# The order of issue planned in the source, w_in by column tile, batch 0's softmax with tokens on partitions

## The chip, the cores and the metric
One core of a Trainium2 chip. The metric is the device time of one execution in microseconds, as the median of several runs; a program that computes something else or in another precision does not count. The engines that matter are PE (TensorE, matmuls, with PEld for its weight loads), DVE (VectorE), ACT (ScalarE), POOL (GpSimd) and SP (SyncE, which issues most DMAs). Each executes its own list of instructions in order and waits on semaphores; the lists are fixed when the program is built.

## The reference
Eight batches b of 512 tokens x and 32 state rows, with 8 heads of width 64. First a two-way attention, then a feed-forward layer with squared ReLU over all 8 x (512 + 32) = 4352 rows of width 512, hidden width 2048; everything in float32.

```python
scores = scale * x @ state.T          # a = softmax over the 32 state rows, xread = a @ state
scores2 = scale * state @ x.T         # a2 = softmax over the 512 tokens, sread = a2 @ x
rows = concatenate([xread, sread])    # heads side by side: 512 columns
h = rows @ w_in; g = relu(h) ** 2; out = g @ w_out
```
The sums of the two softmaxes get 1e-9 before the division.

## The kernel before
**Precision.** A float32 operand of a big matmul is split into a high part (rounded to the type float32r, a copy on ACT, line 98) and a low part (the difference, a subtraction, line 99); three products hi x hi, lo x hi, hi x lo are added in PSUM. The weights come as 64-bit words; `singles` (lines 101 to 115) makes float32 of them with one ACT operation and three DVE operations per 128 x 512 tile.

**Work for the 512 tokens of a batch.** xread @ w_in is a @ (state @ w_in), so the kernel forms z = state @ w_in per head once for four batches together (`z_part`, L142: eight instructions on PE into two PSUM tiles `pz`, two ACT copies L157, one DMA to DRAM `zd`) and fetches the rows of a batch again (`z_fetch`, L179). For the first 6 of the 16 column blocks of batch 0 z is formed directly (`z_direct`, L165, three times 256 columns). A *unit* is one block `fc` of 128 hidden columns of one batch: `up` (L349) multiplies z by the softmax a (6 matmuls of 512 columns, L353) into `ph`, takes ReLU on ACT (L355), squares on ACT for the first ten units and on DVE after that (L357, L359) and splits into g_hi and g_lo; `down` (L366) multiplies by a 128 x 512 tile of w_out (12 matmuls, L379) into four PSUM tiles `po`. `mlp` (L342) runs `up(i)`, then `down(i - 2)`. After the last unit of a batch `po` goes to SBUF tiles `os_` (3 buffers) and out.

**Batch 0 in two visits.** `BOTH` (L67) orders the units: columns 0 to 5 of batch 0, then all of batch 1, then columns 6 to 15 of batch 0, then batches 2 to 7. The sums of the first visit go to DRAM and are added back in the second (L560 to L572).

**Softmax.** `attention_group` (L214), twice per batch (4 heads each): the scores of state row by token (`scores`, L241) lie with (head, state row) on partitions. `soft1` and `soft1b` turn 32 x 32 blocks with a DVE stream transpose (L262), so that the 32 state rows of a head lie along the free axis, take maximum, difference, exponential, sum, reciprocal and product (L274 to L284), turn back (L286) and split into a_hi, a_lo. Difference and product are on POOL for batches 0 to 2, on DVE from batch 3 on (`pool_early(b < 3)`); a_lo is on DVE for batch 0 and POOL after it. The other softmax, e2 (L263 to L268), is kept, and `turn` and `read` (L297, L312) form sread in `sr` two batches later. For batches from 2 on x is split too, low parts on POOL (L238, L294).

**Loads and weights.** 16 tiles of w_in (512 KB, 256 columns and half of the rows each, `z_load`) and 16 tiles of w_out (`wo_load`, L402) share four buffers `raw`; the low part of w_out is made on POOL (L412).

**Last part.** The 256 state rows of all batches go through the same layer with 16 units of half width (L579 to L609).

**Order.** Two lists of steps, `weights` and `reads`, are spread by counting: each has steps with due slots, and after each `up` and each `down` the class `Ahead` (L436) emits as many steps as the nearest due slot needs. The framework then schedules the emitted operations once more with its own timing model (`schedule_with_timeline_sim=True`, L639).

## Time and profile before
| | |
|---|---|
| time, median of 3 runs | 762.25 us (761.93 to 762.26) |
| profiled execution: time, span | 761.69 us, 759.9 us |
| PE busy, mean granted clock | 713.6 us (94%), 0.952 |
| DVE, ACT, POOL busy | 439.1 us (58%), 378.3 us (50%), 151.9 us (20%) |
| DMA | 79.00 MB, mean 104 GB/s |
| chain that ended last | PE 82%, DVE 9%, DMA 4%, ACT 2% |

The share of busy time is an average over stages that differ: some 110 us in which the weights come in, then batch after batch. Busy PE is not PE at full speed: the row of the granted clock says what share of the full clock it had. A line number such as L99 can be that of a helper (`split`, `singles`), so groups are told apart by the tiles they write.

### The profile page before, as it was taken

The numbers are of one execution on the slowest core, as the hardware profiler recorded it, in microseconds if no ns is written. First come the engines' busy times: TensorE is split into PE (matmuls) and PEld (weight loads), VectorE is DVE, ScalarE is ACT, GpSimd is POOL, SyncE is SP. The second block draws the span as 40 slices with busy tenths as digits, with TensorE's granted clock in tenths as the row PEclk, the third lists the DMA queues.
The fourth block names the chain that finished last, engine by engine and source line by source line (L and its number), as shares of the span: only waits on it lengthen the run. The fifth ranks groups of instructions, "written<-read, shape, count | busy, mean of one in ns | idle before, by whom it ended". The sixth has DMA issues, their size and how long they took to land.

```text
span 759.9 us, 9457 instructions
## 1 busy us (share of the span) xinstructions
PE 713.6 (94%) x3136; PEld 561.3 (74%) x3136; DVE 439.1 (58%) x729; ACT 378.3 (50%) x714; POOL 151.9 (20%) x170
## 2 busy tenths in 40 slices
PE   4899669999998999996999999999999999999997
PEld 2556447777885777764888888888888888888896
DVE  5999852334565432636477588478468544444453
ACT  4486664334555544644465565466446434533443
POOL 1333240000323120113223222223312211100000
PEclk9599769999997999995999999999999999999999
DMA  9577870033225333242132321141113201200101
GB/s 306 196 252 264 306 258 27 28 125 124 70 63 200 108 106 138 84 152 85 36 90 58 115 83 57 56 138 56 61 60 119 81 28 39 73 28 1 56 1 28
DMA packets 50368, 79.00 MB, mean 104 GB/s; under 512 B 6928, under 2 KB 32656, under 8 KB 50320
## 3 DMA queue, kind: packets, MB, share of 16 engines
q1 hardware_dynamic: 45520, 61.37, 25.0%
q10 hardware_dynamic: 4800, 17.04, 5.7%
q8 instruction: 24, 0.39, 0.2%
q14 instruction: 24, 0.20, 0.1%
HBM read 51.64 MB, written 26.74 MB: 103 GB/s over the span
## 4 chain that ended last, share of the span: by engine, by line
PE 82%; DVE 9%; DMA 4%; ACT 2%; issue 2%; POOL 0%; SPq 0%; DVEq 0%; ACTq 0%; POOLq 0%
PE po L379 47%; PE ph L353 25%; PE pz L151 4%; PE pr L316 2%; PE pst L257 1%; PE pq L247 1%; DMA w_raw<-w_in 1%; DVE wof L112 1%; DVE wof L108 1%; DVE wi L108 1%; DMA part<-os__634 1%; PE pt L304 1%; DVE wi L112 1%; DMA part<-os__646 1%; DMA sp_f<-stP 1%
## 5 line engine op out<-in xcount | busy, mean ns | idle before, releaser
L379 PE MATMUL po<-wo_hi,g_hi 128*128 128x512 f32 x544 | 219.2, 403 | 6.5 <-ACT g_hi L98 6.5
L379 PE MATMUL po<-wo_lo,g_hi 128*128 128x512 f32 x544 | 215.9, 397 | 0.0
L359 DVE TENSOR_TENSOR ph<-ph,r 128x512 f32<-128x512 f32 (+1 forms) x134 | 89.0, 665 | 178.5 <-ACT r L355 178.1
L355 ACT ACTIVATE r<-ph 128x512 f32<-128x512 f32 (+1 forms) x144 | 82.6, 576 | 193.6 <-PE ph L353 193.6
L379 PE MATMUL po<-wo_hi,g_lo 128*128 128x512 f32 x544 | 151.7, 394 | 0.0
L379 PEld LDWEIGHTS po<-wo_hi,g_hi 128*128 128x128 f32 x544 | 103.5, 190 | 33.9 <-ACT g_hi L98 7.8
L99 DVE TENSOR_TENSOR g_lo<-ph,g_hi 128x512 fp32r<-128x512 f32 (+1 forms) x144 | 94.5, 658 | 58.5 <-ACT g_hi L98 33.9
L379 PEld LDWEIGHTS po<-wo_lo,g_hi 128*128 128x128 f32 x544 | 103.7, 191 | 21.8 <-issue 0.3
L379 PEld LDWEIGHTS po<-wo_hi,g_lo 128*128 128x128 f32 x544 | 101.2, 188 | 22.3 <-issue 0.8
L98 ACT CAST g_hi<-ph 128x512 fp32r<-128x512 f32 (+1 forms) x144 | 81.0, 564 | 50.1 <-DVE ph L359 37.5
L99 POOL TENSOR_TENSOR xn_hl<-xn_raw,xn_hl 128x512 fp32r<-128x512 f32 x32 | 42.3, 1321 | 223.6 <-ACT xn_hl L98 223.6
L353 PE MATMUL ph<-a_hi,z_hi 128*128 128x512 f32 x256 | 85.4, 412 | 0.8 <-ACT a_hi L98 0.7
L353 PE MATMUL ph<-a_hi,z_lo 128*128 128x512 f32 x256 | 84.1, 411 | 0.0
L353 PE MATMUL ph<-a_lo,z_hi 128*128 128x512 f32 x256 | 82.7, 404 | 0.0
L151 PE MATMUL pz<-wi,st_z 64*128 64x256 f32 x256 | 63.2, 446 | 13.6 <-ACT z_stage L157 12.8
L151 PEld LDWEIGHTS pz<-wi,st_z 64*128 64x128 f32 x256 | 38.1, 207 | 37.0 <-ACT z_stage L157 18.8
L99 POOL TENSOR_TENSOR xt_hl<-xt_raw,xt_hl 128x512 fp32r<-128x512 f32 x24 | 31.5, 1312 | 161.7 <-ACT xt_hl L98 161.7
L353 PEld LDWEIGHTS ph<-a_hi,z_lo 128*128 128x128 f32 x256 | 50.9, 199 | 12.2 <-issue 0.7
L353 PEld LDWEIGHTS ph<-a_lo,z_hi 128*128 128x128 f32 x256 | 49.6, 195 | 12.8 <-issue 1.7
L353 PEld LDWEIGHTS ph<-a_hi,z_hi 128*128 128x128 f32 x256 | 48.6, 196 | 13.9 <-issue 1.6
L157 ACT COPY z_stage<-pz 128x512 f32<-128x512 f32 x64 | 36.5, 588 | 32.7 <-PE pz L151 30.1
L99 DVE TENSOR_TENSOR z_lo<-z_raw,z_hi 128x512 fp32r<-128x512 f32 x61 | 44.9, 735 | 8.3 <-ACT z_hi L98 8.3
(120 smaller groups left out, 706.7 us busy)
## 6 DMA issues: line engine op xcount, KB each, us to landing
zd<-z_stage ACTq DMA_DIRECT2D x32, 512.0 KB, 3.0
z_raw<-zd SPq DMA_DIRECT2D x244, 64.0 KB, 2.3
xt_raw<-xT SPq DMA_DIRECT2D x16, 512.0 KB, 3.6
w_raw<-w_in SPq DMA_DIRECT2D x16, 512.0 KB, 4.8
wo_raw<-w_out SPq DMA_DIRECT2D x16, 512.0 KB, 4.9
xn_raw<-xn SPq DMA_DIRECT2D x16, 512.0 KB, 3.8
part<-part SPq DMA_DIRECT2D x4, 256.0 KB, 3.2
st_z<-stT SPq DMA_DIRECT2D x4, 128.0 KB, 5.6
```

The lines of the kernel that those rows point to most:

```text
L98: nc.scalar.copy(out=hi, in_=src)
L99: eng_lo.tensor_sub(out=lo, in0=src, in1=hi.bitcast(F32))
L108: nc.vector.scalar_tensor_tensor(out=bits, in0=high, scalar=-0x80000000, in1=bits, op0=ALU.bitwise_and, op1=ALU.bitwise_or,)
L112: nc.vector.scalar_tensor_tensor(out=bits, in0=low, scalar=29, in1=bits, op0=ALU.logical_shift_right, op1=ALU.bitwise_or,)
L151: nc.tensor.matmul(pz[i][:, q, :], lhsT=st[G][own, cc, :], rhs=wi[own, k, cc, :], start=True, stop=True,)
L157: nc.scalar.copy(out=stage[:, :, i, :], in_=pz[i])
L247: nc.tensor.matmul(pq, lhsT=sp_hl[:, g, q].rearrange("p i n -> p (i n)"), rhs=v, start=i == 0, stop=i == 1,)
L316: nc.tensor.matmul(pr[:, q].rearrange("p i c -> p (i c)"), lhsT=my["e"][:, t, q].rearrange("p i n -> p (i n)"), rhs=my["xn"][q][:, t].rear ...
L353: nc.tensor.matmul(ph, lhsT=w, rhs=v, start=i == 0, stop=i == len(todo) - 1)
L355: nc.scalar.activation(r, ph, AF.Relu)
L359: nc.vector.tensor_mul(out=ph, in0=ph, in1=r)
L379: nc.tensor.matmul(po[t], lhsT=g, rhs=w, start=i == 0 and j == 0, stop=i == last and j == 2)
```

## The change
The order of every instruction on every engine is now worked out in the source. Each step is declared to a `Planner` with its engine (or a choice of engines), an assumed duration, the tiles that it reads and writes, and for some a due time; due times are passed back from consumers to producers. `run` then steps through a model time: of the operations that could begin first on an engine (within 0.02 us) it takes the one with the earliest due time. The framework's own scheduler is off. The model knows that a DVE operation with `both` waits for POOL's end, and takes DMA as one queue at 360 GB/s plus 2.2 us. No operation is dropped from the units; other differences:

- w_in comes in 16 tiles of 128 columns and all rows, so one tile serves one unit; z for batch 0's first six blocks is formed per 128 columns.
- Batch 0's softmax over state rows has its scores computed a second time with tokens on partitions (`sT`, 8 products a group), so no stream transposes; the result is turned back by PE (`pa`, 4 transposes). The scores for e2 (`pst`) begin at 22 us of model time at the earliest. `PARTS` keeps the two visits.
- Difference, product and a_lo: DVE for batch 0, DVE or POOL for batch 1, POOL from batch 2 on. The low part of w_out: DVE. The square and the copies of `po`: ACT or DVE, as the plan finds.
- `down` of a unit is due 7.8 us after its `up`, a unit's step being 4.4 us.

```diff
+    def run(self):
+        for o in reversed(self.ops):
+            cost = o.engs[0][1] + o.lat + (o.size / self.RATE + self.LAND if o.size else 0.0)
+            for s_ in o.succ:
+                o.due = min(o.due, s_.due - cost)
+            if o.next is not None:
+                o.due = min(o.due, o.next.due)
+            if o.hold is not None:
+                o.begin = max(o.begin, o.due - o.hold)
...
+                now = free.get(e, 0.0)
+                first, able = 1e18, []
+                for o in cs:
+                    t = max(now, o.ready, o.begin)
...
+                t, o = min(((t, o) for t, o in able if t <= first + 0.02), key=lambda to: to[1].due)
+                if best is None or t < best[0]:
+                    best = t, e, o
...
+            o.run(e)
+            end = t + cost
+            if e == "POOL":
+                pool_end = end
+            elif o.both and e == "DVE":
+                end = max(end, pool_end + cost)
+            free[e] = end
+            if o.size:
+                queue = max(queue, end) + o.size / self.RATE
+                o.end = queue + self.LAND
+            else:
+                o.end = end + o.lat
...
+def pe(n, k=1):
+    return ("PE", k * (0.0134 + n / 2400))
+
+
+def act(n):
+    return ("ACT", 0.05 + n / 1200)
+
+
+def dve(n):
+    return ("DVE", 0.07 + n / 960)
+
+
+def dve2(n):
+    return ("DVE", 0.07 + n / 1920)
+
+
+def gps(n):
+    return ("POOL", 0.15 + n / 450)
...
+    DIRECT = 6
     PLAIN_X = 2
-    BOTH = ((0, 6), (1, NFC), (0, NFC))
-    LATE = 2
-    XHL = 1
-    GUARD = 2.0**-112
-
-    def pool_early(early):
-        return nc.gpsimd if early else nc.vector
+    PARTS = [(0, 0, 6), (1, 0, NFC), (0, 6, NFC)] + [(b, 0, NFC) for b in range(2, B)]
+    START, FIRST, STEP = 18.0, 4.8, 4.4
...
+        raw=4, xraw=2, x_hl=1, z_stage=2, st_z=1, z_raw=2, z_hi=2, z_lo=2, a_hi=2, a_lo=2,
+        sp_raw=2, st=1, at=1, st_low=1, q1=2, e2=4, s2=4, nm2=2, m1=2, s1=2, e_hl=1, both=1, low=1,
+        r=2, g_hi=2, g_lo=2, os_=3, wof=2, po=4, ph=2, px=2,
...
+    units = [(b, fc) for b, lo, hi in PARTS for fc in range(lo, hi)]
+    when = [START + FIRST * min(u, NFC) + STEP * max(0, u - NFC) for u in range(len(units) + 1)]
...
+    def split(hi, lo, src, n, r, wh, wl, engs=None, due=1e9, both=True, chain=None):
+
+        op(act(n), lambda e: nc.scalar.copy(out=hi(), in_=src()), r=r, w=wh, due=due, chain=chain)
+        op(
+            engs or [dve(n)],
+            lambda e: ENGINE[e].tensor_sub(out=lo(), in0=src(), in1=hi().bitcast(F32)),
+            r=[*r, *wh], w=wl, due=due, both=both,
+        )
...
+    def load(out, in_, size, r=(), w=(), due=1e9, begin=0.0, hold=45.0, issue=0.42, eng="SP", chain=None):
+        op(
+            (eng, issue), lambda e: ENGINE[e].dma_start(out=out(), in_=in_()),
+            r=r, w=w, size=size, due=due, begin=begin, hold=hold, chain=chain,
+        )
...
+    def w_tile(fc):
+        raw = tile_([P, NCC, P, 2], I32, "w_raw", "raw")
+        load(lambda: raw.t.rearrange("p c f w -> p (c f w)"), lambda: w_in[fc], 512, w=[raw])
+        singles(lambda: wi[:, fc], lambda: raw.t, [raw], [("wi", fc)])
...
+                        lhsT=sp_f[:, g].rearrange("p q n -> p (q n)")[:, q * P:(q + 1) * P],
+                        rhs=wi[:, fc, g * NQ + q, :], start=q == 0, stop=q == NQ - 1,
+                    )
+
+        op(("PE", 0.95), product, r=["sp_f0", "sp_f1", ("wi", fc)], w=[pz])
...
+    def two_source(n, b):
+        return [[dve(n)], [dve(n), gps(n)]][b] if b < 2 else [gps(n)]
...
+        turned = b == 0
+        if turned:
+            sT = tile_([P, NJ, N], F32, "sT", "po")
+
+            def product_t(e):
+                for t in range(NT):
+                    for q in range(NQ):
+                        nc.tensor.matmul(
+                            flat(sT.t)[:, t * P + q * 2 * N:t * P + (q + 1) * 2 * N],
+                            lhsT=xt.t[:, q, t * P:(t + 1) * P], rhs=sp_f[:, g, q, :2 * N],
+                            start=True, stop=True,
+                        )
+
+            op(("PE", 1.6), product_t, r=["sp_f0", "sp_f1", xt], w=[sT])
+            src = sT
...
+            def turn_back(e):
+                for t in range(NT):
+                    nc.tensor.transpose(
+                        out=at.t[:, t * P:(t + 1) * P], in_=flat(q1.t)[:, t * P:(t + 1) * P], identity=ident
                     )
-            q1 = sb.tile([P, NJ, N], F32, name="q1", bufs=2)
-            nc.vector.transpose(out=q1.rearrange("p j n -> p (j n)"), in_=pst)
-            nm2 = sb.tile([P, 1], F32, name="nm2", bufs=2)
-            nc.vector.tensor_reduce(out=nm2, in_=pst, axis=AX.X, op=ALU.max, negate=True)
-            nc.scalar.mul(nm2, nm2, SCALE)
-            e2 = sb.tile([P, S], F32, name="e2", bufs=2 * LATE)
-            s2 = sb.tile([P, 1], F32, name="s2", bufs=2 * LATE)
-            nc.scalar.activation(e2, pst, AF.Exp, bias=nm2, scale=SCALE, accum_out=s2)
-            my.update(e2=e2, s2=s2, q1=q1)
-
-        def soft1():
-            q1 = my["q1"]
-            m1 = sb.tile([P, NJ, 1], F32, name="m1", bufs=2)
-            nc.vector.tensor_reduce(out=m1[:, :, 0], in_=q1, axis=AX.X, op=ALU.max)
-            pool_early(b < 3).tensor_sub(out=q1, in0=q1, in1=m1.broadcast_to([P, NJ, N]))
-            nc.scalar.activation(q1, q1, AF.Exp, scale=SCALE)
-
-        def soft1b():
-            q1 = my["q1"]
-            s1 = sb.tile([P, NJ, 1], F32, name="s1", bufs=2)
-            nc.vector.tensor_reduce(out=s1[:, :, 0], in_=q1, axis=AX.X, op=ALU.add)
-            nc.vector.tensor_scalar_add(s1, s1, EPS)
-            nc.vector.reciprocal(s1, s1)
-            pool_early(b < 3).tensor_mul(out=q1, in0=q1, in1=s1.broadcast_to([P, NJ, N]))
-            at = sb.tile([P, S], F32, name="at", bufs=2)
-            nc.vector.transpose(out=at, in_=q1.rearrange("p j n -> p (j n)"))
-            split(pair[0][:, g, :], pair[1][:, g, :], at, pool_early(b))
-
-        def cut_n():
-            raw = my["n"].rearrange("p t (q c) -> p t q c", c=P)
-            my["xn"] = []
-            for q in range(NQ):
-                hl = sb.tile([P, NT, 2, P], F32R, name="xn_hl", tag="x_hl", bufs=XHL)
-                split(hl[:, :, 0, :], hl[:, :, 1, :], raw[:, :, q, :], nc.gpsimd)
-                my["xn"].append(hl)
-
-        def turn():
-            s2 = my["s2"]
-            nc.vector.tensor_scalar_add(s2, s2, EPS)
-            nc.vector.reciprocal(s2, s2)
-            nc.vector.tensor_scalar_mul(my["e2"], my["e2"], s2)
-            pt = ps_x.tile([P, NT, P], F32, name="pt", tag="px")
+
+            op(("PE", 0.6), turn_back, r=[q1], w=[at])
...
+        split(
+            lambda: wo[k][0][:, i, :], lambda: wo[k][1][:, i, :], lambda: wf.t, DM,
+            [wf], [("wo", 0, fc)], [("wo", 1, fc)],
...
+        op([dve(width), act(width)], square, r=[ph, rl], w=[ph])
...
+        order = [(t, j) for t in range(nt) for j in range(3)]
+        if last:
+            todo = [[x for x in order if x[0] == t] for t in range(nt)]
         else:
-            nc.vector.tensor_copy(out=dst, in_=po)
-
-    def wo_load(fc):
+            todo = [[x for x in order if x[1] < 2], [x for x in order if x[1] == 2]]
+            if first:
+                todo[:1] = [[x for x in todo[0] if x[0] == t] for t in range(nt)]
...
+    pad(0)
+    for g in range(NG):
+        scores(0, g)
+    for m in range(NFC):
+        w_tile(m)
+        if m < DIRECT:
+            z_direct(m)
+        wo_tile(m)
+    z_state(0)
+    for m in range(NFC):
+        z_part(0, *divmod(m, NG))
...
+    for b, lo, hi in PARTS:
+        if b not in started:
+            pad(b)
+            for g in range(NG):
+                scores(b, g)
+            started.add(b)
+        if lo == 0 and b >= 1:
+            for g in range(NG):
+                read(b - 1, g, begins[b] + 8 * STEP)
+        if b == 2 and not z1[0]:
+            z1[0] = True
+            z_state(1)
+            for m in range(NFC):
+                z_part(1, *divmod(m, NG), begin=begins[2] + m * (begins[GB] - begins[2]) / (NFC + 4) - 5)
...
+            g_ = up(fc, S, todo, r, 3 * NG * pe(S)[1], when[u])
+            down(po, fc, g_, fc == lo, fc == hi - 1, when[u] + 2 * STEP - 1)
...
-            np.ascontiguousarray(moe_w_in).view(np.int64).reshape(2, -1, 128, DF // 256, 256)
-            .transpose(3, 0, 2, 1, 4)
-        ).reshape(DF // 256 * 2, 128, -1),
+            np.ascontiguousarray(moe_w_in).view(np.int64).reshape(-1, 128, DF // 128, 128)
+            .transpose(2, 1, 0, 3)
+        ).reshape(DF // 128, 128, -1),
...
-    with tile.TileContext(nc, schedule_with_timeline_sim=True) as tc:
+    with tile.TileContext(nc, schedule_with_timeline_sim=False) as tc:
```

More of the change, by code (lines that the diff above doesn't have):

```diff
@@ L536, in aux @@
[L536 to L553 removed]
+                        in0=both.t[i * N:(i + 1) * N, q, i * D:(i + 1) * D],
@@ L590, in first @@
[L590 to L603 removed]
+                (w.t[:, cc, :], v.t[:, cc, :])
```

906 lines of the change are left out of this document (534 added, 372 removed).

## Prediction
> **What bounds the kernel now.** I read the table of stages first, with cuts put where the slices of the page change. Columns: stretch, its length, then for PE, the weight loads, DVE, ACT and POOL the busy time with the count, the granted TensorE clock, DMA share, GB/s.
>
> ```profile
> span 759.9 us, 9457 instructions
> ```
> ```profile
> 0.00:112.00 112.00, 82.96 (x257) 52.35 (x258) 93.18 (x158) 67.90 (x128) 38.38 (x35) 0.82 0.78 264
> 112.00:230.00 118.00, 117.25 (x516) 93.17 (x516) 50.55 (x77) 50.20 (x91) 14.01 (x17) 0.98 0.23 77
> 230.00:260.00 30.00, 26.96 (x101) 18.61 (x100) 15.15 (x27) 16.59 (x33) 10.06 (x11) 0.83 0.50 184
> 260.00:340.00 80.00, 79.76 (x356) 59.69 (x354) 32.75 (x53) 38.70 (x70) 9.12 (x10) 1.00 0.32 112
> 340.00:372.00 32.00, 23.89 (x90) 18.86 (x89) 18.07 (x30) 14.40 (x29) 10.22 (x14) 0.73 0.22 76
> 372.00:752.00 380.00, 380.00 (x1813) 316.65 (x1812) 227.90 (x384) 189.45 (x363) 70.07 (x83) 1.00 0.19 60
> 752.00:760.00 8.00, 2.82 (x13) 1.97 (x11) 1.55 (x3) 1.05 (x3) 0.00 (x0) 0.88 0.24 66
> ```
> From 372 to 752 us PE is busy without a gap at full clock, so no order of issue can win there. Busy time times clock is the full-speed work a stage got, and the rest of the stage is lost: 112 - 82.96 x 0.82 = 44.0 us up to 112, 3.1 us up to 230, 30 - 26.96 x 0.83 = 7.6 us up to 260, 32 - 23.89 x 0.73 = 14.6 us up to 372, 5.5 us in the tail. That is 75 us in all, and only this can be won.
>
> The price of one unit (one block of 128 hidden columns of one batch) is read off two successive pieces of the chain of waits (start, length, what), and the number of units done by 112 us off the groups of the first stage.
>
> ```profile
> 675.69 2.75 PE po L379 x12
> 679.81 2.75 PE po L379 x12
> ```
> ```profile
> L379 PE MATMUL po<-wo_hi,g_hi 128*128 128x512 f32 x25 | 11.5, 461 | 3.9 <-ACT g_hi L98 3.9
> L353 PE MATMUL ph<-a_hi,z_hi 128*128 128x512 f32 x16 | 7.3, 521 | 0.1
> ```
> A unit is 679.81 - 675.69 = 4.12 us of PE. Four of the first kind belong to a unit, so 25 mean 6 units through the second matmul by 112 us; two of the second kind, so 8 units begun. Why so few is told by the chain of waits in that stage, which runs through DVE's weight conversion and, four times, through a transfer:
>
> ```profile
> 67.21 3.41 DMA w_raw<-w_in
> 71.72 6.07 DMA w_raw<-w_in
> ...
> 86.62 5.90 DMA part<-os__634
> 93.21 5.37 DMA part<-os__646
> ```
> 9.5 us go to late weight tiles, 11.3 us to batch 0's partial sums on their way to DRAM, behind which ACT stands in order. DVE is busy 93.18 of 112 us.
>
> **The first unit.** Three rows of the timeline (start, length, instruction) and one of the weight loads of the score product (min/median/max ns):
>
> ```profile
> 2.25 1.33 SPq L200 DMA_DIRECT2D sp_f<-stP  x2
> ...
> 8.25 6.51 PE L257 MATMUL pst<-xt_raw,sp_f 128*128 128x512 f32 x8 [8.25 <-DMA sp_f<-stP]
> ...
> 32.48 1.65 PE L353 MATMUL ph<-a_hi,z_hi 128*128 128x512 f32 x3
> ```
> ```profile
> L257 PEld LDWEIGHTS pst<-xt_raw,sp_f x16: 187/337/338, 8.2 to 73.1; 128*128 128x128 f32 x16
> ```
> The small state load is issued at 2.25 us behind two x loads and one weight tile on SP's queue. The planner gives it the due time of the first score product, which I expect to put it behind one x load, so that a third of the bytes stand ahead of it: of the 6.0 us from issue to product 2 to 6 remain, which makes 4.5 to 8.25 us; I take 6. The turned scores are 4 x 2 products a group, and as the float32 score product shows two instructions each (8 for four products), 16 short ones with a weight load each. 64 columns stream faster than the weights load, so I price them by the weight load: 16 x 0.337 = 5.4 us, or 3.0 us at the minimum. Two groups end at 6 + 10.8 = 16.8 us. Behind the second: maximum, subtract, sum, multiply and low part on DVE (5 x 0.69, see below), exponential and high part on ACT (2 x 0.6, as its rows further down), and some 1.1 for reciprocal and four transposes, an estimate: 5.8 us. The first unit begins at 22.6, say 23 us, against 32.48: 9.5 us earlier. Bounds: 18 (fast weight loads), 26 (DVE in the middle of a weight tile, three operations). The pst product moves behind 22 us into the units' time, but it was on PE before them already. Direct z by column tile has 48 products of half width instead of 24; they lie in the wait for the softmax, and half of them after the first unit, at most 24 x 0.337 - 24 x 0.21 = 3 us, inside the bounds below.
>
> **DVE in the load stage, 20 to 110 us.** Groups of that stretch (count | busy us, mean ns | idle before), and the durations of one kind over the run:
>
> ```profile
> L112 DVE SCALAR_TENSOR_TENSOR wof<-wo_raw,wof 128x512 int32<-128x512 int32 x16 | 13.6, 848 | 0.1
> L112 DVE SCALAR_TENSOR_TENSOR wi<-w_raw,wi 128x512 int32<-128x512 int32 x13 | 11.1, 856 | 0.0
> L108 DVE SCALAR_TENSOR_TENSOR wi<-w_raw,wi 128x512 int32<-128x512 int32 x12 | 10.1, 843 | 0.0
> L301 DVE TENSOR_SCALAR e<-e,s 128x512 f32<-128x512 f32 x4 | 2.9, 719 | 0.0
> L286 DVE STREAM_TRANSPOSE at<-q 128x512 f32<-128x512 f32 x4 | 2.8, 702 | 2.4 <-POOL q L284 2.4
> L99 POOL TENSOR_TENSOR wo_lo<-wof,wo_hi 128x512 fp32r<-128x512 f32 x16 | 22.5, 1405 | 35.5 <-ACT wo_hi L98 35.5
> ```
> ```profile
> L112 DVE SCALAR_TENSOR_TENSOR wi<-w_raw,wi x16: 623/690/1773, 9.7 to 89.1; 128x512 int32<-128x512 int32 x16
> ```
> The conversions' median is 0.69 us and their means in this stretch 0.84 to 0.86, with single ones at 1.77: they stand while POOL works on wo_lo. Leaving out POOL's wo_lo saves 16 x 0.158 + 13 x 0.166 + 12 x 0.153 = 6.5 us; batch 0's four stream transposes go (2.8), the four scalings of e move out of the stage (2.9): 12.2 us less. Added: 16 low parts of w_out on DVE (16 x 0.69 = 11.0) and batch 0's two subtracts and two multiplies (2.8): 13.8 us more. So DVE's demand stays as it is, +1.6 us, and a gain must come out of its idle 112 - 93.18 = 18.8 us. One more unit takes DVE g_lo, half a z_lo and perhaps the square, 1.0 to 1.7 us; five take 5 to 9 us, which fits. PE sets the cap: of the 44.0 us lost some 14 stay (23 us to the first unit less about 9 us of products in it: 2 x 3.0 for the turned scores and 3 for z, at full clock), 30 us are 7 units. I take 9.5 us for the earlier start and half of the 20.8 us of transfer waits, together 19.9 us, 5 units, **-20.6 us**; bounds 0 and -29. The transfers carry the same bytes, so I expect half of the waits to survive. The tiles by column cost nothing: the same 512 KB each; what they hide behind is the softmax chain to 23 us, and without that cover one tile (two operations of 0.69 us and a shorter shift on DVE) would still be one less in front of the first unit.
>
> The Trainium skill (SBUF — State Buffer, section "SBUF: two separate sides") says that DVE operations with two SBUF inputs and GpSimd share an exclusive port pair, and that the loser waits for the whole instruction. By that rule the 22.5 us of wo_lo on POOL would block DVE up to 22.5 us instead of the 6.5 us that the means show; DVE would gain up to 16 us more, the load stage would go to its cap, and the sum would be about 8 us lower, near 720. The trace agrees with the kind (a conversion of 1773 ns), not with the size, so the sum goes by the means.
>
> **The stalls at 230 to 260 and 340 to 372 us.** Pieces of the chain:
>
> ```profile
> 347.67 1.43 DVE q L284
> ...
> 350.55 4.22 PE ph L353 x9
> ```
> The next batch's units wait for its softmax, which DVE reaches late, among a store of old work. A due time worked back from the batch's start would issue it earlier; what is late next is the read of the batch before, due half a batch later. With the cold 3.1 us after 112 the stalls lost 25.3 us. Bounds 0 (they turn up elsewhere) and -25.3; a planner that knows the due times but not the real durations should get 60%: **-15 us**.
>
> **POOL instead of DVE from batch 3 on.** Groups of the whole run:
>
> ```profile
> L284 DVE TENSOR_TENSOR q<-q,s 128x512 f32<-128x512 f32 x10 | 9.6, 957 | 0.3
> L284 POOL TENSOR_TENSOR q<-q,s 128x512 f32<-128x512 f32 x6 | 7.6, 1261 | 11.2 <-DVE s L283 6.5 <-ACT wof L104 4.7
> L275 DVE TENSOR_TENSOR q<-q,m 128x512 f32<-128x512 f32 x10 | 6.8, 684 | 0.0
> L275 POOL TENSOR_TENSOR q<-q,m 128x512 f32<-128x512 f32 x6 | 6.5, 1083 | 24.2 <-DVE m L274 22.8 <-DVE s L299 1.4
> ```
> 16.4 us leave DVE, 23.4 us come to POOL. Both are hidden: in the 380 us of full PE DVE has 152 us free, POOL 310. Zero.
>
> **One unit of lookahead.** Before, the second matmul of unit u follows the first of u+2; by the due times it now follows that of u+1. Steps of one unit:
>
> ```profile
> 700.51 0.60 ACT L355 ACTIVATE r<-ph 128x512 f32<-128x512 f32 x1 [2.16 <-PE ph L353]
> 701.14 0.70 DVE L359 TENSOR_TENSOR ph<-ph,r 128x512 f32<-128x512 f32 x1 [2.07 <-ACT r L355]
> ...
> 701.88 0.59 ACT L98 CAST g_hi<-ph 128x512 fp32r<-128x512 f32 x1 [0.77 <-DVE ph L359]
> ```
> From 700.51 to 702.47 are 1.96 us; PE has 4.12 us of other work meanwhile. Slack 2.2 us, against at most three operations of 0.7 us queued ahead of the steps. If the cover fails, PE stands for the difference. I take **+2 us** for the run; bounds 0 and the slower rival's price.
>
> **Sum.** The profiled execution took 761.69 us, 1.8 more than its span; 761.69 - 20.6 - 15 + 2 = 728.1. The median of the runs, 762.25, lies 0.6 above: 728.7, rounded to 728.5.
>
> **Rivals.** (a) *All of it works*: the load stage at its cap, no stall left: 762.25 - 29 - 25.3 = 708. For it: each engine is idle somewhere in every stalled stage; against: the first stage has DVE at 83% and DMA at 78%. (b) *Late transfers stay in the way.* The planner lands 512 KB in 512/360 + 2.2 = 3.6 us; the issue list shows
>
> ```profile
> w_raw<-w_in SPq DMA_DIRECT2D x16, 512.0 KB, 4.8
> ```
> so ACT's in-order queue may meet loads 1.2 us early, thirty-two times, and keep the 20.8 us. Then 762.25 - 9.5 - 15 + 2 = 740. (c) *Slower*: the one-unit lookahead. Some 122 units are left after 112 us; it decides from 35.6 / 122 = 0.29 us of stall a unit on. At 0.4 us it costs 49 us: 762.25 - 35.6 + 49 = 775.5. And short gaps cost more than themselves:
>
> ```profile
> 230.00:240.00 10.00, 7.52 (x32) 4.62 (x31) 8.17 (x16) 6.77 (x15) 3.59 (x3) 0.96 0.65 242
> 240.00:250.00 10.00, 10.00 (x28) 6.91 (x27) 1.31 (x4) 3.22 (x6) 3.62 (x3) 0.53 0.42 164
> ...
> 238.41 6.03 PE L151 MATMUL pz<-wi,st_z 64*128 64x256 f32 x16 [1.35 <-ACT z_stage L157]
> ```
> After 2.5 us of gaps in 10 us, the one before 238.41 being 1.35 us, PE ran the next 10 us at 0.53 of its clock. Against it: 2.2 us of slack.
>
> The Trainium skill (TensorE: Matmul & The Clock Gate, section "What's actually happening") puts the return to half clock after an idle window of about 3.4 us. By it gaps of 0.4 us cost no clock and (c) stays at 775; by the row here denser gaps halve the clock, and (c) would be worse than that. (d) *It doesn't do what it says*: the order differs, but DMA at 264 GB/s and DVE keep the load stage as long, and the stalls only move: 762.
>
> **Chances.** Forecast (716 to 736) 0.46, (a) 0.16, (b) 0.21, (c) 0.12, (d) 0.05. About 0.2% is what runs of this kernel tell from no change. Faster 0.46 + 0.16 + 0.21 = 0.83, same 0.05, slower 0.12. The range leaves out (c), and (a) where it goes beyond 704, some 0.05: 704 to 761. The likeliest case alone has 716 to 736.
>
> **What would show it.** The first ph matmul near 23 us; about 44 po<-wo_hi,g_hi matmuls (11 units) by 112 us; no DMA piece over 3 us between 60 and 100 us in the chain; stages after 230 us with PE over 97% and clock 1.00; ACT's r and g_hi rows without PE waiting for them in the last 380 us. Wrong if PE waits for g_hi in the steady stage (c), if DVE's conversions still have means over 0.8 us, or if the clock stays under 0.8 up to 100 us.

## The result and the profile after

The changed kernel takes 705.64 us (median; 704.69 to 706.44) against 762.09 us (761.79 to 762.26): a ratio of 0.9259, 95% interval 0.9243 to 0.9275, 56.4 us less. The profiled execution took 705.21 us; its span is 56.4 us shorter than that of the kernel before, too.

The table of stages of the changed kernel, with the cuts of the prediction (stretch, its length, busy time and count of PE, weight loads, DVE, ACT and POOL, granted clock, DMA share, GB/s):

```profile
span 703.5 us, 9460 instructions
```
```profile
0.00:112.00 112.00, 91.20 (x401) 68.52 (x402) 88.14 (x166) 69.79 (x133) 18.36 (x26) 0.94 0.67 229
112.00:230.00 118.00, 117.30 (x543) 93.41 (x542) 73.72 (x125) 81.15 (x154) 30.38 (x30) 1.00 0.42 137
230.00:260.00 30.00, 30.00 (x143) 25.02 (x143) 12.29 (x22) 15.57 (x27) 9.07 (x10) 1.00 0.27 80
260.00:340.00 80.00, 80.00 (x378) 62.59 (x377) 37.02 (x65) 50.35 (x95) 18.65 (x21) 1.00 0.35 113
340.00:372.00 32.00, 32.00 (x155) 25.24 (x154) 11.10 (x17) 16.51 (x30) 4.06 (x6) 1.00 0.33 108
372.00:697.00 325.00, 325.00 (x1581) 270.87 (x1580) 148.19 (x254) 187.71 (x360) 67.13 (x77) 1.00 0.20 67
697.00:704.00 7.00, 1.84 (x9) 1.18 (x7) 0.00 (x0) 1.17 (x2) 0.00 (x0) 0.91 0.27 75
```

Lost again means length less busy time times clock. Up to 112 us that gives 112 - 91.20 x 0.94 = 26.3 us, against 44.0; up to 230 us 0.7 against 3.1; from 230 to 372 us nothing against 22.4; in the tail 6.5 - 1.84 x 0.91 = 4.8 against 5.5.

The first stage needs a correction in both kernels. The column of the clock says 1.00 up to the first change that the trace records, at 13.98 us in the kernel before and at 26.88 us in the changed one, but the instructions show half speed there. The eight instructions of the score product `pst` show it: from 8.25 us on they take 6.51 us in the kernel before (a row of the prediction), with starts 0.85 us apart up to 13.5 us and 0.43 us apart after 14 us. In the changed kernel they come behind the first change (start, length, piece of the chain):

```profile
29.49 3.43 PE pst L464 x8
```
Ahead of its first change PE is busy for 5.73 us in the kernel before and for 15.77 us in the changed one. Half of that is lost as well, 2.9 and 7.9 us, so the load stage loses 46.9 us before and 34.2 us after. Together 39.7 us are lost against 77.9, so 38.2 us of the 56.4 come from less standing and less low clock. The other **18.2 us** must be work that PE now does in less time at full clock: 759.9 - 77.9 = 682.0 us of it before, 703.5 - 39.7 = 663.8 after. No operation was dropped, and some were added.

Where these 18.2 us are is seen when one kind of PE work is followed through both traces. I added up, for every matmul, the time from its start to the start of the next one on PE, by the tile it writes:

```
us, all instructions of the kind    before   after
pz  (256, z_part)                     74.9    36.9
ph  (960)                            214.8   202.3
po  (1631)                           385.1   388.3
pst (16)                              11.0     6.1
pr, pt, pq, pzd                       60.4    44.6
sT, pa (new)                             -    14.0
all                                  746.2   692.2
```
38 of the 54 us stand beside the 256 pz instructions, whose number and size did not change. Part of that was waiting and low clock, which the stages count already. To take both out I counted for each instruction the time to the next start, less PE's idle time in it, times the clock (half ahead of the first recorded change). Then pz has 51.8 us before and 34.2 after: 17.6 us less, nearly all of the 18.2. All other PE work is the same in sum, 629.5 us before and 629.4 after. Where the 17.6 us are shows in the timeline (start, length, instruction). Kernel before:

```profile
276.53 1.13 PE L151 MATMUL pz<-wi,st_z 64*128 64x256 f32 x4
277.58 0.38 PE L316 MATMUL pr<-xn_hl,e_hl 128*128 128x256 f32 x1
...
288.25 1.14 PE L151 MATMUL pz<-wi,st_z 64*128 64x256 f32 x8
289.32 0.50 PE L379 MATMUL po<-wo_hi,g_hi 128*128 128x512 f32 x1
```
Changed kernel:

```profile
330.86 1.13 PE L357 MATMUL pz<-wi,st_z 64*128 64x256 f32 x8
331.93 0.50 PE L714 MATMUL po<-wo_hi,g_hi 128*128 128x512 f32 x1
```
A z_part has eight instructions, four on state rows 0 to 63 and four on rows 64 to 127. All eight together hold PE for 1.07 us (288.25 to 289.32, 330.86 to 331.93); four of one half alone hold it for 1.05 us (276.53 to 277.58). In the kernel before eight instructions stand by themselves in only ten places: seven whole z_parts and, by PE's list, three times the second half of one z_part beside the first half of the next, which take 1.07 us as well. 92 instructions, 11.5 z_parts, are in pieces of 2, 4 or 6 among other work, and the rest in five long runs; in the changed kernel all 32 z_parts are whole. PE counts as busy in both cases.

### The profile page after: what moved, and what is told of

Read it like the earlier page. It is cut to its first block, busy times and chain, and to the rows that moved or that the text cites. A ratio compares the mean times of both kernels' runs of the same rounds, so it can differ in the third digit from the quotient of the medians.

```text
span 703.5 us, 9460 instructions
## 1 busy us (share of the span) xinstructions
PE 677.3 (96%) x3200; PEld 546.8 (78%) x3200; DVE 370.4 (53%) x646; ACT 422.2 (60%) x799; POOL 147.6 (21%) x170
## 4 chain that ended last, share of the span: by engine, by line
PE 86%; DMA 7%; DVE 2%; ACT 2%; issue 1%; SPq 0%; POOL 0%; ACTq 0%; POOLq 0%
PE po L714 50%; PE ph L678 26%; PE pz L357 3%; DMA z_raw<-zd 2%; PE pr L619 2%; DMA zd<-z_stage 2%; PE pq L486 2%; DMA xn_raw<-xn 1%; PE pzd L387 1%; PE sT L514 1%; PE pt L601 1%; DMA w_raw<-w_in 1%; DMA wo_raw<-w_out 1%; DVE wi L314 1%; DMA sp_f<-stP 1%
## 5 line engine op out<-in xcount | busy, mean ns | idle before, releaser
L714 PE MATMUL po<-wo_lo,g_hi 128*128 128x512 f32 x544 | 213.6, 393 | 0.0
L714 PE MATMUL po<-wo_hi,g_lo 128*128 128x512 f32 x544 | 153.6, 393 | 0.6 <-DVE g_lo L288 0.6
L692 DVE TENSOR_TENSOR ph<-ph,r 128x512 f32<-128x512 f32 (+1 forms) x65 | 44.3, 682 | 127.9 <-ACT r L684 127.9
L678 PE MATMUL ph<-a_hi,z_hi 128*128 128x512 f32 x256 | 81.0, 398 | 1.8 <-ACT z_hi L285 1.8
L678 PE MATMUL ph<-a_hi,z_lo 128*128 128x512 f32 x256 | 80.1, 394 | 0.0
L678 PE MATMUL ph<-a_lo,z_hi 128*128 128x512 f32 x256 | 79.7, 393 | 0.0
L678 PEld LDWEIGHTS ph<-a_hi,z_hi 128*128 128x128 f32 x256 | 48.4, 191 | 12.7 <-ACT z_hi L285 2.4
L678 PEld LDWEIGHTS ph<-a_hi,z_lo 128*128 128x128 f32 x256 | 48.7, 191 | 11.2 <-DVE z_lo L288 0.9
L690 ACT ACTIVATE ph<-r 128x512 f32<-128x512 f32 (+1 forms) x79 | 45.1, 571 | 1.9
L365 ACT COPY z_stage<-pz 128x512 f32<-128x512 f32 x64 | 34.8, 590 | 10.8 <-PE pz L357 10.8
L285 ACT CAST z_hi<-z_raw 128x512 fp32r<-128x512 f32 x61 | 37.5, 615 | 4.2 <-DMA z_raw<-zd 4.0
```

Of the source, the lines that this page charges most:

```text
L285: op(act(n), lambda e: nc.scalar.copy(out=hi(), in_=src()), r=r, w=wh, due=due, chain=chain)
L365: act(512), lambda e, i=i: nc.scalar.copy(out=stage.t[:, :, i, :], in_=pz[i].t),
L678: nc.tensor.matmul(ph.t[:, :width], lhsT=w, rhs=v, start=j == 0, stop=j == len(pairs_) - 1)
L690: nc.scalar.activation(ph.t[:, :width], rl.t[:, :width], AF.Square)
L692: nc.vector.tensor_mul(out=ph.t[:, :width], in0=ph.t[:, :width], in1=rl.t[:, :width])
L714: nc.tensor.matmul(po[t].t, lhsT=(g[0], g[0], g[1])[j].t[:, t * P:(t + 1) * P], rhs=wo[k][j % 2][:, i, :], start=first and j == 0, stop=la ...
```

## The experiments

The theory after these readings: the 56 us are the load stage (up to 112 us, 12.7 us), the stalls from 112 to 372 us (24.8 us) and the pairs of half-row products (17.6 us). Rivals: the pairs do nothing and something else goes with the order; the new layouts and batch 0's softmax carry the gain, not the order. All runs are compared with the kernel before on the same chip, which took 761.0 to 761.5 us beside them. For each run the table gives the time, the ratio with its interval, the time lost by stage as above, and the two sums from start to next start. The first stage is counted with half speed ahead of the first recorded change; the expectations count it without, as 17.7 us won, with 26.3 us lost in the changed kernel and 15.6 and 16.9 in e2 and e7. In the last stage of e8 and e10 the clock is taken to four digits, since 3.41 us of it ran at half speed.

| kernel | us | ratio (95%) | lost 0-112 | 112-230 | 230-372 | 372-690 | pz | all PE |
|---|---|---|---|---|---|---|---|---|
| before | 762.1 | 1 | 46.9 | 3.1 | 22.4 | 0 | 74.9 | 746.2 |
| changed | 705.6 | 0.926 (0.924-0.928) | 34.2 | 0.7 | 0 | 0 | 36.9 | 692.2 |
| e3 half after half | 706.6 | 0.929 (0.926-0.932) | 37.4 | 0.5 | 0 | 0.3 | 37.8 | 696.3 |
| e5 reordered | 739.8 | 0.972 (0.968-0.977) | 32.8 | 0.3 | 0 | 0 | 71.0 | 726.8 |
| e10 halves apart | 735.5 | 0.968 (0.963-0.972) | 22.5 | 0 | 0.8 | 6.3 | 66.4 | 721.3 |
| e1 no turned softmax | 704.9 | 0.926 (0.923-0.930) | 30.3 | 3.9 | 0 | 0 | 41.7 | 693.2 |
| e2 row tiles | 699.3 | 0.920 (0.916-0.924) | 21.7 | 3.3 | 0.7 | 0 | 42.0 | 684.6 |
| e6 wo_lo on POOL | 708.3 | 0.932 (0.928-0.935) | 32.5 | 1.2 | 0.3 | 1.1 | 43.4 | 695.7 |
| e11 all three undone | 717.4 | 0.944 (0.941-0.946) | 30.0 | 15.3 | 0 | 0.2 | 48.8 | 704.0 |
| e7 longer lookahead | 699.3 | 0.920 (0.916-0.923) | 25.1 | 3.0 | 0 | 0 | 38.5 | 687.4 |
| e12 e2 with e7 | 697.5 | 0.917 (0.914-0.919) | 20.8 | 1.2 | 0 | 0 | 37.3 | 685.1 |
| e8 reads later | 704.5 | 0.926 (0.923-0.929) | 23.0 | 3.1 | 0 | 4.8 | 41.1 | 691.4 |
| e9 measured figures | 710.3 | 0.933 (0.930-0.936) | 27.8 | 9.7 | 0 | 0.6 | 44.7 | 697.2 |

### Are the pairs the missing work?

**e3: one half after the other.**

```diff
-            for q in range(NQ):
-                for i in range(2):
+            for i in range(2):
+                for q in range(NQ):
                     own = slice(i * D, (i + 1) * D)
```


> The changed kernel, with one edit: in z_part the loop over the two halves of 64 state rows is outside and the loop over the four products inside, so that four products of one half follow one another before the other half begins. The number of instructions, their sizes and the plan's assumed time stay. Theory of pairs: two neighbouring instructions on rows 0-63 and 64-127 run at once (their starts lie 13 ns and 202 ns apart in the traces so far), and a half alone lasts as long as the pair, so each of the 32 z_parts becomes 0.43 to 0.85 us longer: 705.6 + 14 to 705.6 + 27 us, about 725, and the eight instructions of a z_part last 1.5 to 2.1 us from first start to next in place of 1.06. Rival (order of the halves is indifferent, the long z_parts of the kernel before came from its waits): 705.6, within 1 us.

Measured: 706.63 us, within a microsecond of the changed kernel. The theory as written there fell. The timeline of e3:

```profile
328.63 1.14 PE L357 MATMUL pz<-wi,st_z 64*128 64x256 f32 x8
329.70 0.50 PE L714 MATMUL po<-wo_hi,g_hi 128*128 128x512 f32 x1
```
The eight still hold PE for 1.07 us, although four of one half stand ahead of four of the other in PE's list, and their starts still come two by two, 13 or 14 ns apart. So the order inside a z_part does not matter. That leaves two readings: only neighbourhood counts, at any distance within the eight, or pairs have nothing to do with it.

**e5: the same steps, order left to the framework.**

```diff
-    with tc.manual_schedule():
-        plan.run()
+    plan.run()
...
-    with tile.TileContext(nc, schedule_with_timeline_sim=False) as tc:
+    with tile.TileContext(nc, schedule_with_timeline_sim=True) as tc:
```


> The changed kernel with the plan's order handed to the framework's own scheduler with its timing model, as in the kernel before, in place of fixing it: same instructions, same loads, same softmax, other order. Theory (the order that the plan fixes is worth the stalls, some 25 us, and the pairs of half-row products, 14 us or more): 735 to 760, with idle PE between 230 and 380 us or z_part products apart from their partners. Rival (the gain lies in the tiles, batch 0's softmax and the choice of engines, whatever fixes the order): 704 to 712.

Measured: 739.8 us, 34.2 above the changed kernel. The table of stages of e5, and its timeline:

```profile
0.00:112.00 112.00, 89.89 (x372) 66.10 (x373) 97.24 (x182) 69.57 (x136) 17.86 (x22) 0.94 0.74 255
112.00:230.00 118.00, 117.67 (x510) 90.15 (x509) 53.56 (x87) 70.04 (x133) 28.50 (x31) 1.00 0.31 103
230.00:372.00 142.00, 142.00 (x616) 108.92 (x616) 67.33 (x112) 79.09 (x148) 31.91 (x35) 1.00 0.28 94
372.00:690.00 318.00, 317.97 (x1439) 256.73 (x1438) 145.84 (x237) 175.10 (x324) 70.90 (x83) 1.00 0.23 73
```
```profile
359.43 1.13 PE L357 MATMUL pz<-wi,st_z 64*128 64x256 f32 x4
360.49 0.50 PE L714 MATMUL po<-wo_lo,g_hi 128*128 128x512 f32 x1
...
363.20 1.13 PE L357 MATMUL pz<-wi,st_z 64*128 64x256 f32 x4
364.26 0.73 PE L678 MATMUL ph<-a_hi,z_hi 128*128 128x512 f32 x2
```
This is the most telling run. No stall came back: PE is as busy in every stage as in the changed kernel, within 1.4 us, at the same clock. Yet 34 us are gone, with fewer matmuls through in the same busy time (616 against 672 from 230 to 372 us). The sum over all PE work is 34.6 us longer, and the pz instructions alone 34.1. At 359.43 and 363.20 each half takes 1.06 us by itself. My expectation had idle PE as one of two marks; only the other, products apart from their partners, came true.

**e10: halves declared apart.**

```diff
-        op(("PE", 1.2), product, r=[...], w=pz, begin=begin)
+        for i in range(2):
+            op(
+                ("PE", 0.6), lambda e, i=i: product(i),
+                r=[..., (st[G], i), *([("half", G, k, g)] if i else [])],
+                w=[pz[i], *([] if i else [("half", G, k, g)])], begin=begin, lat=0.2 if i else 2.5,
+            )
```


> The changed kernel with each z_part declared as two steps, one for each half of 64 state rows, the second not before 2.5 us of model time after the first; the order is planned again. Same instructions. In PE's list the 64 halves then stand in 52 places, 43 of them a half alone among other work, where the changed kernel has 32 whole z_parts. Theory (what counts is that the partner half is a neighbour in PE's list, at any distance within the z_part; a half alone takes the 1.06 us of a whole z_part): the pz instructions take 52 x 1.06 = 55 us and some 3 us at low clock in place of 36.9, so the time goes to 705.6 + 15 to 705.6 + 23, 720 to 729, most likely 726, with PE busy all the while. Rival (the 34 us between the changed kernel and the one that the framework reordered come from something else that goes with its order): 704 to 710.

Measured: 735.47 us, 29.8 above the changed kernel; the pz instructions take 66.4 us, 29.5 more. The size is larger than expected, for a reason that serves as a control. The timeline of e10:

```profile
304.01 1.13 PE L356 MATMUL pz<-wi,st_z 64*128 64x256 f32 x4
305.07 0.50 PE L718 MATMUL po<-wo_hi,g_hi 128*128 128x512 f32 x1
...
426.17 1.99 PE L356 MATMUL pz<-wi,st_z 64*128 64x256 f32 x8
428.09 1.21 PE L718 MATMUL po<-wo_hi,g_lo 128*128 128x512 f32 x4
```
At 304.01 a half alone holds PE for 1.06 us. At 426.17 two halves are neighbours, but in PE's list both are halves of rows 64 to 127, of two z_parts: 1.92 us. I had counted such neighbours as pairs. So eight neighbours take 1.07 us when they are of opposite row halves and 1.92 us when they are of the same. That the halves run side by side, and that this is worth the 30 us, is shown by e3, e5 and e10 together. With idle time and low clock taken out, pz has 62.4 us in e5 and 65.1 in e10 against 34.2; the other PE work has 636.6 and 633.4 against 629.4. The stages of e10 shift beside that: it loses 22.5 us up to 112 us in place of 34.2, and 6.3 us after 372 us.

The Trainium skill (TensorE: Matmul & The Clock Gate, section "The mechanism") says that matmuls in different row groups of the array overlap; the 1.07 against 1.92 us here agree. Its section "Step-by-step: what each phase is for" says that the matmuls themselves stay in program order and only weight loads are pulled ahead. By that e3 should have taken longer; it did not, and the measurement decides.

**e4: the kernel before, with its halves alternating.** 
```diff
+            with tc.manual_schedule():
                 for q in range(nq):
                     for i in range(2):
                         ...
                         nc.tensor.matmul(
```


> The kernel before, with one edit: the framework may not reorder the eight instructions of a z_part, so that the two halves of 64 rows alternate as written. Theory of pairs: of the 38 us by which the 256 pz instructions were slower in the kernel before (74.9 against 36.9 us, start to next start), the part outside the load stage comes back: -10 to -20 us, 742 to 752. If pairs do nothing: 762, within 3 us for a plan that shifts a little. If the fixed group hinders the framework's scheduler elsewhere (it may no longer fill gaps with single products): above 762.

Measured: 771.71 us against 761.22, ratio 1.0143 (1.0118 to 1.0169), the last case of the expectation. The edit held the order of the eight, but not their neighbourhood: its z_parts mostly stand in pieces of 2 and 6. With idle time and low clock taken out, pz has 45.9 us against 51.8, so a part of the pairs did come back; but the load stage lost 112 - 74.74 x 0.82 = 50.7 us and 1.7 more ahead of the first recorded change, 52.4 against 46.9, and from 230 to 372 us 31.0 us are lost against 22.4. Why pinning a few instructions hinders that scheduler elsewhere was not followed up.

### What carries the load stage?

**e1: batch 0's softmax like the others.** 
```diff
-                begin=0.0 if b else START + 4.0,
+                begin=0.0,
...
-        turned = b == 0
+        turned = False
```


> The changed kernel without one part: batch 0's softmax over state rows is made as in the other batches (scores by state row, stream transposes on DVE) and its pst product may begin at once; the order is planned again. Theory (the turned softmax is part of the earlier first unit): the first ph matmul moves from 24.2 to 29-33 us and the end by 5 to 9 us, 711 to 715. Rival 1 (the load stage is set by loads and weight conversion, not by the first unit): first unit later, but time 704 to 707. Rival 2 (the turned softmax is where most of the 56 us is from): above 725.

Measured: 704.91 us, not to be told from the changed kernel. The timeline of e1:

```profile
5.96 6.34 PE L464 MATMUL pst<-xt_raw,sp_f 128*128 128x512 f32 x8 [5.96 <-DMA sp_f<-stP]
...
28.22 0.80 PE L678 MATMUL ph<-a_hi,z_hi 128*128 128x512 f32 x2
```
The first unit is 4.3 us later (28.22 against 23.89) and nothing is lost by it: the sT and pa products are not there, and pst, which the changed kernel makes among the units (6.1 us), lies in the wait instead. The first rival fits: set against its price, the turned softmax buys nothing. What the earlier start alone is worth is not shown, since e1 takes away both.

**e2: w_in by row halves and 256 columns.** `w_tile` loads and converts the tile of the kernel before, `z_part` reads one tile, `z_direct` two, in pairs of blocks.

```diff
-        raw = tile_([P, NCC, P, 2], I32, "w_raw", "raw")
+        k, g = divmod(fc, NG)
+        raw = tile_([P, NQ, FW, 2], I32, "w_raw", "raw")
...
-        op(("PE", 1.2), product, r=[("wi", k * FPC + i) for i in range(FPC)] + [(st[G], 0), (st[G], 1)], w=pz, begin=begin)
+        op(("PE", 1.2), product, r=[("wi", k, g)] + [(st[G], 0), (st[G], 1)], w=pz, begin=begin)
...
-        op(("PE", 0.95), product, r=["sp_f0", "sp_f1", ("wi", fc)], w=[pz])
+        op(("PE", 0.95), product, r=["sp_f0", "sp_f1", ("wi", k, 0), ("wi", k, 1)], w=[pz])
...
-        if m < DIRECT:
+        if m % NG and m < DIRECT:
+            z_direct(m - 1)
             z_direct(m)
```


> The changed kernel without one part: w_in comes in tiles of 256 columns and half of the rows as in the kernel before (same bytes for each tile, direct z in pairs of column blocks); the order is planned again. Theory (tile form costs one more tile ahead of the first unit and one more held back at each pair): +2 to +6 us, 708 to 712. Rival 1 (hidden behind the softmax chain, as the prediction had it): 704 to 707. Rival 2 (the form of the tiles is where most of the gain of the load stage is from): +15 us or more.

Measured: 699.31 us, 6.3 us faster than with tiles by column. No theory had that sign. From the first recorded change at 23.05 us on, the first stage of e2 ran at full clock (the 1.00 of this row counts the time ahead of it as full speed):

```profile
0.00:112.00 112.00, 96.43 (x460) 73.42 (x461) 96.73 (x183) 77.24 (x147) 19.81 (x26) 1.00 0.72 248
```
21.7 us are lost there in place of 34.2, 6.1 of them ahead of that change. A z_part needs one tile of this form and two of the other; that this is why was not tried by itself.

**e6: the low part of w_out on POOL.**

```diff
-            [wf], [("wo", 0, fc)], [("wo", 1, fc)],
+            [wf], [("wo", 0, fc)], [("wo", 1, fc)], engs=[gps(DM)],
```


> The changed kernel with the low part of w_out on POOL again in place of DVE, the order planned again. By the prediction's balance (DVE gets rid of 16 x 0.69 = 11.0 us and gets 6.5 us of waiting for POOL back): -4 to 0, 702 to 706. If DVE is the bound of the load stage and a POOL subtraction makes it stand for the whole 1.4 us (16 x 1.4 = 22.5 us less 11): +5 to +11, 711 to 717. If the load stage is bound elsewhere: 704 to 707.

Measured: 708.31 us, 2.7 above the changed kernel, intervals just apart (0.9276 to 0.9353 and 0.9243 to 0.9275); between the first two theories.

**e11: e1, e2 and e6 together,** so that of the new parts order and choice of engines remain.

> The changed kernel without three of its parts at once: w_in in tiles of 256 columns and half of the rows, batch 0's softmax as in the other batches, the low part of w_out on POOL, all as in the kernel before; the order is planned in the source. Theory (order and pairs carry all of the gain, the other three parts none): 699 to 710. Rival 1 (the parts can stand in for one another, so that one alone taken away shows nothing, but together they carry the 17.7 us that the load stage won): 715 to 725. Rival 2 (they carry more than half of the gain): above 733.

Measured: 717.35 us, 11.7 above the changed kernel, 44.1 below the kernel before: the first rival. Its losses have moved to the end of the loads, as three rows of its stage table show:

```profile
110.00:120.00 10.00, 7.04 (x32) 5.07 (x31) 10.00 (x13) 3.85 (x8) 6.58 (x7) 0.86 0.79 276
120.00:130.00 10.00, 8.76 (x22) 4.49 (x21) 8.52 (x12) 7.53 (x15) 5.71 (x4) 0.50 0.42 144
130.00:140.00 10.00, 9.11 (x29) 5.93 (x30) 7.54 (x13) 6.49 (x14) 3.57 (x3) 0.62 0.36 133
```
30 - 7.04 x 0.86 - 8.76 x 0.50 - 9.11 x 0.62 = 13.9 us are lost in 30, most of it by low clock. DVE is the engine without a gap at 110 us, and its conversions are slow beside POOL's work. Groups of DVE from 20 to 130 us (count | busy us, mean ns | idle before), changed kernel:

```profile
L314 DVE SCALAR_TENSOR_TENSOR wof<-wo_raw,wof 128x512 int32<-128x512 int32 x16 | 12.1, 754 | 0.1
L308 DVE SCALAR_TENSOR_TENSOR wi<-w_raw,wi 128x512 int32<-128x512 int32 x15 | 10.2, 688 | 0.0
```
and e11:

```profile
L314 DVE SCALAR_TENSOR_TENSOR wof<-wo_raw,wof 128x512 int32<-128x512 int32 x15 | 12.4, 828 | 0.1
L308 DVE SCALAR_TENSOR_TENSOR wi<-w_raw,wi 128x512 int32<-128x512 int32 x14 | 13.7, 997 | 0.0
```
So up to 230 us the kernel before lost 50.0 us, e11 45.3, the changed kernel 34.9: the three parts together carry 10.4 of the 15.1 us won there, while with one of them alone taken away 34.2 (e1), 25.0 (e2) and 33.7 (e6) are lost, no more than in the changed kernel. Which two of them can do without the third was not tried.

### Lookahead, reads, figures of the plan

**e7: the second matmul due one step later.**

```diff
-            down(po, fc, g_, fc == lo, fc == hi - 1, when[u] + 2 * STEP - 1)
+            down(po, fc, g_, fc == lo, fc == hi - 1, when[u] + 3 * STEP - 1)
```


> The changed kernel with the second matmul of a unit due one step (4.4 us) later, so that it may follow the first matmul of the unit after the next, as in the kernel before. If one unit of lookahead leaves no stall, as the trace after the change has it: 704 to 707. If single waits for g_hi or g_lo in the load stage come from the short lookahead: -2 to -5, 700 to 704. If two buffers of g_hi and ph then hold up the first matmul: +2 to +10.

Measured: 699.3 us, 6.3 below. From 230 us on it is like the changed kernel; the load stage loses 25.1 us in place of 34.2. One unit of lookahead costs nothing where PE is full, and something where the weights come in, if the difference is not the new plan's. That it was waits for g_hi or g_lo there is not shown: the changed kernel has only 1.4 us of them (below).

**e8: reads of x held back.**

```diff
-            512, w=[xr], due=due, chain="x",
+            512, w=[xr], due=due, begin=due - 25.0, chain="x",
```


> The changed kernel, with the loads of x for sread (xn_raw, 256 KB and more each) held back until 25 us before their due time in place of 45. In the trace of the changed kernel one of them lands 9.06 us after its issue, in the chain of waits at 54 to 63 us. Theory (such a transfer takes bandwidth from weight tiles and partial sums in the load stage): -1 to -5 us, 700 to 704. Rival (another transfer takes its place, or DVE and ACT set the stage): 704 to 707. If reads then come too late for their own due times: above 708.

Measured: 704.45 us, no difference. The load stage did gain (23.0 in place of 34.2 us lost), but 2.4 us were lost again up to 230 us and 4.8 after 372 us, where PE now waits 2.9 us for the low parts of x (`xn_hl`) and runs at half clock for 3.41 us: 7.2 us given back of 11.2 won. The rest lies in a longer tail and in PE work.

**e9: measured figures in the plan.**

```diff
-    RATE = 360.0
-    LAND = 2.2
+    RATE = 300.0
+    LAND = 3.0
...
-    return ("ACT", 0.05 + n / 1200)
+    return ("ACT", 0.16 + n / 1200)
```
and DVE 0.08 in place of 0.07.

> The changed kernel with the planner's assumed durations moved towards the traces: DMA at 300 GB/s plus 3.0 us in place of 360 and 2.2, ACT 0.16 us in place of 0.05 ahead of the stream, DVE 0.08 in place of 0.07; the order is planned again. Rival (b) of the prediction (loads and stores that land later than the plan knows leave engines standing in order): -3 to -10 us, 696 to 703, with fewer transfers of over 3 us in the chain up to 112 us. If the plan's order is not sensitive to its figures: 703 to 708.

Measured: 710.28 us, 4.6 slower, above both ranges. The plan does not get better by figures nearer to the traces: 6.4 us fewer are lost up to 112 us and 9.0 more up to 230.

**e12: e2 and e7 together,** the fastest kernel of this study.

> The changed kernel with the two edits that made it faster by 6 us each: tiles of 256 columns and half of the rows, and the second matmul of a unit due one step later. If each takes away a cause of its own in the load stage (15.6 and 16.9 us lost there in place of 26.3): 690 to 696. If both reach the same limit of that stage, or a new plan is a new throw of dice within some 6 us: 697 to 704.

Measured: 697.54 us, ratio 0.9169 (0.9144 to 0.9194), 8 us below the changed kernel, below e2 and e7 by less than their intervals tell apart. The gains do not add up: three different edits (e2, e7, e12) leave 20.8 to 25.1 us lost up to 112 us. Whether that is a limit of the stage or the scatter of new plans is not shown.

## Why the prediction was right or wrong

The forecast of 728.5 had the direction. The measured 705.64 us lie in its range of 704 to 761, though 1.6 us from its end and below the likeliest 716 to 736. It is near the time of rival (a), 708, which had a chance of 0.16, but not made up as (a) had it: less was won in the load stage, and 18.2 us came from a term that no case had. That the range still held is luck.

| term | predicted | measured |
|---|---|---|
| load stage up to 112 us | -20.6 | 46.9 to 34.2: -12.7 |
| stalls 112 to 372 us | -15 | 25.5 to 0.7: -24.8 |
| lookahead | +2 | 0 from 230 us on |
| tail | 0 | -0.7 |
| PE work at full clock | 0 | 682.0 to 663.8: -18.2 |
| sum | -33.6 | -56.4 |

**The step that failed** is "That is 75 us in all, and only this can be won", with "Busy time times clock is the full-speed work a stage got" behind it. I took busy time times clock for work that must be done. It held half-row products without their partners: the order changed how long the same 256 instructions hold PE, and no view of stalls shows that. The rows were in reach: the z_part products from one start to the next, 1.05 us for four and 1.07 us for eight. The pz instructions of the kernel before all stand ahead of 340 us; so "no order of issue can win there", said of the stage from 372 us on, is not what failed. A second slip is in the same sum: it took the clock ahead of 13.98 us as full, which left out 2.9 us.

**The stalls** were mis-sized, right in kind: I took 60%, and all of it went (PE 100% at clock 1.00 from 230 to 697 us). The reason, a planner that knows the due times "but not the real durations", was a bad one; e9, with figures nearer to the traces, is slower. Nor is a fixed order needed for it: e5 has no stall either, nor has e11, without the three parts. What e5 and e11 share is the steps with their due times, but also the new choice of engines: from 372 to 690 us DVE is busy for 197.9 us in the kernel before and for 145.8 to 147.5 us in e5, e11 and the changed kernel. No run keeps the old choice of engines with the new due times, so which of the two removes the stalls stays open. Fixing the order gave the pairs.

**The load stage** came out near the forecast in units (forecast 11 by 112 us), but with 12.7 us less lost where I had 20.6. The units also hold what was put off: 96 of the pz instructions stand ahead of 112 us in the kernel before, 72 in the changed one. Groups of the changed kernel up to 112 us, and its first timeline rows:

```profile
L714 PE MATMUL po<-wo_hi,g_hi 128*128 128x512 f32 x43 | 18.5, 430 | 0.9 <-ACT g_hi L285 0.8
L678 PE MATMUL ph<-a_hi,z_hi 128*128 128x512 f32 x24 | 9.3, 475 | 1.1 <-ACT z_hi L285 1.1
```
```profile
6.28 7.06 PE L514 MATMUL sT<-sp_f,xt_raw 128*128 128x64 f32 x32 [6.28 <-DMA sp_f<-stP]
16.23 2.08 PE L387 MATMUL pzd<-wi,sp_f 128*128 128x128 f32 x8 [2.89 <-DVE wi L314]
...
23.89 1.20 PE L678 MATMUL ph<-a_hi,z_hi 128*128 128x512 f32 x2
```
43 make 10.75 units, 24 make 12 begun. The state load landed for a start at 6.28 us (forecast 6), and the first unit began at 23.89 (forecast 23). Inside, two errors nearly cancel: the turned scores took 7.06 us for 32 instructions, 0.22 each, where I took 0.337 and 10.8 us; and from their end to the first unit 23.89 - 13.34 = 10.6 us passed where I took 5.8, with direct z on PE in between and its wait of 2.89 us for DVE's conversion, which I had hidden. But the use made of it, "9.5 us for the earlier start", did not hold: PE ran at half speed up to 26.88 us, and e1 gives 4.3 us of that start back, drops the added products and ends at the same time. The pst product "was on PE before them already", I wrote; before, it lay in the wait, and moved among the units it costs 6.1 us. Nor is "The tiles by column cost nothing" borne out: the plan without them is 6.3 us faster, though that may be the plan's.

**The transfer waits** did not go. The chain of waits of the changed kernel (start, length, what):

```profile
53.90 9.06 DMA xn_raw<-xn
...
72.55 6.20 DMA wo_raw<-w_out
78.76 5.37 DMA z_raw<-zd
...
92.54 6.44 DMA w_raw<-w_in
```
"No DMA piece over 3 us between 60 and 100 us" was wrong three times over, with the load stage nonetheless near its forecast in units. Such pieces in a chain are what ended last, and their length is not what the time would gain: e8 moved the longest of them, the stage lost 11.2 us less, and the end came at the same time. I had read the chain of the kernel before in the same way.

**DVE's balance** held. The conversions came down to 0.69 to 0.76 us in the rows above, and POOL's wo_lo put back (e6) costs 2.7 us. Its conversions from 20 to 130 us take 47.3 us in all, against 44.7 in the changed kernel. The rule of the Trainium skill (SBUF — State Buffer, section "SBUF: two separate sides") that DVE can be locked out for the whole of a POOL instruction would allow up to 22.5 us more; no run here shows so much.

**Rival (c)**, stalls by the short lookahead, did not come about. Two groups of the whole run of the changed kernel:

```profile
L714 PE MATMUL po<-wo_hi,g_hi 128*128 128x512 f32 x544 | 217.6, 400 | 0.9 <-ACT g_hi L285 0.8
L714 PE MATMUL po<-wo_hi,g_lo 128*128 128x512 f32 x544 | 153.6, 393 | 0.6 <-DVE g_lo L288 0.6
```
PE waited 0.8 us for g_hi and 0.6 us for g_lo in the whole run, all of it in the load stage. The slack was enough. **Rival (b)** asked whether the plan's DMA figures cost time; with figures nearer to the traces e9 is slower.

## What to carry to other kernels

A busy engine at full clock is not an engine at its work: before calling a stage full, compare how long one and the same group of instructions holds the engine at different places, from start to next start. Products on half of the rows are worth issuing as one inseparable group with their partners on the other half; here a scheduler that placed them one by one gave about 30 us away (e5). Fixing their order alone is not enough (e4): they must stay neighbours. And where a planner makes the order, one part taken away tells little, since the next plan can make up for it; take several away together, and count a difference of a few microseconds between two plans as theirs, not as the edit's. Where a record of the clock has no entry yet, compare like instructions early and late before taking it for full speed.

## What the runs showed of the hardware

Four instructions of 64 x 256 on one half of the rows hold PE for 1.06 us, eight on both halves for 1.07 us, eight on the same half for 1.92 us. The partner is found even when four instructions of the first half stand ahead of it in the list (e3: 1.07 us, starts 13 to 14 ns apart). So it is not true of PE that it starts its list strictly in order. The prediction had none of this, and the expectation of e3 had the last of it the other way.

After a stage with gaps the clock stays low beyond them: in e11, after 2.96 us of idle PE between 110 and 120 us, the next 20 us ran at 0.50 and 0.62, with 1.24 and 0.89 us of gaps in them.

The executions begin at half clock, which the column of the clock does not show: the same eight score products take 6.51 us from 8.25 us on in the kernel before, 6.34 us from 5.96 us on in e1, and 3.43 us from 29.49 us on in the changed kernel.
